# Clustered attention and a maxout network on one core: clusters counted for four heads at once with tokens on partitions, a wide mask, and later gathers

## The chip, the cores and the metric

One core of a Trainium2 chip runs the whole program. The metric is device time in microseconds (us), shown as the median of three runs with the lowest and the highest beside it. The profile is one execution on the same chip, recorded by the hardware profiler; its span runs from the first to the last instruction.

## The reference

```python
# B, H, S, D = 4, 8, 768, 64; C = 16 centroids per head
q_assign = argmax(normalize(q) @ normalize(centroids).T)      # per head, per token
k_assign = argmax(normalize(k) @ normalize(centroids).T)
mask = q_assign[:, :, :, None] == k_assign[:, :, None, :]
scores = where(mask, q @ k.T / sqrt(D), -1e9)
x = softmax(scores) @ v            # 4 x 8 x 768 x 64 -> 3072 x 512 by token
h = maximum(maximum(x @ w1, x @ w2), x @ w3)                  # 512 -> 768
out = h @ w_out                                              # 768 -> 512
```

A query meets only the keys of its own cluster. A head has 16 clusters over 768 tokens.

## The kernel before

**What it computes with.** Each head's tokens are sorted by cluster into eight blocks of 128 places; two clusters share a block, the one of rank r by size and the one of rank 15 - r, one from the block's front and one from its back, so that queries meet keys in eight blocks of 128 x 128 and not in the full 768 x 768. If two clusters that share a block have more than 128 tokens, a flag is set, and a second kernel that does without sorting runs behind it; with the inputs used here it does not. Float32 numbers are carried as pairs of 16-bit ones (a high and a low part).

**Stages of a pair of heads** (`pair_units`). `load_x` (L334 to L339) brings q and k of two heads, transposed, into `stage`. `cluster_scores` (L350) multiplies them by the centroids in a two-bank PSUM tile `big`. `best` (L354 to L370) turns 32 x 32 squares with DVE (L356) and finds each token's cluster as a one-hot row, then counts tokens per cluster. `count` (L373 to L421) is a chain that alternates: TensorE sums counts across partitions (L375, L376, L394, L407, L408, L413 to L415, L419) into one bank of `one`, and DVE makes ranks, mates and the start of each cluster from them in small steps. `places` (L423 to L456) gives each token its place, and copies places between partitions (L450). `fences` (L458 to L468) makes two mask tables. `scales` and `splits` (L472 to L512) scale and split the rows of q, k and v. `scatter` (L515, L518) is twelve indirect DMAs issued by GpSimd (POOL): rows of k and v go to their places in a DRAM buffer, one of a ring of three.

**Stages of a head.** The blocks come back from DRAM as kt (transposed) and vt (L537 to L539). `order_q` (L556, L558, L566) sorts q: DVE makes a one-hot matrix `hot` of 128 x 1024 for each of six tiles, TensorE multiplies, ACT copies to `qt`. `scores` (L580 on) makes, in a `big` tile, for each of eight blocks two matmuls of q by the two parts of k (L587, L588) and one of three rows that adds the mask (L589); DVE takes the row maxima (L591), ACT the exponentials (L596) and a 16-bit copy (L600), DVE the remainder (L601), SP transposes it by DMA into `pt`. `values` multiplies by v (L615 to L617), DVE divides (L620), SP writes `o` to one of three DRAM buffers (L622), and POOL gathers it back into token order with six indirect DMAs (L626), into `xb`.

**The network.** A batch's `xb` is scaled and split (`x_split`, split16 at L237 and L238) and transposed. `ffn_units` makes 18 hidden groups of twelve matmuls (L670), twice a batch, each in a bank of `one`, evicted by ACT (L680) or DVE (L682), and three output groups of 18 matmuls (L702), twice a batch. There are 144 hidden and 24 output groups in the run.

**PSUM** has eight banks: two `big` tiles of two banks each (cluster scores, ordered q, scores), and four of `one` (counts, scales, values, the network).

**What sets the order.** Each unit is put into a plan by head, with a priority, by the numbers in the loop at the end (from L730). The tile scheduler then emits instructions for each engine by these priorities and by its own timeline. A pair's count has a priority of three heads ahead of it, read-back and ordering 1.2 heads ahead. The network of a batch is spread over the eight heads of the next one, and the last batch's runs behind the last head. On each engine instructions run in the emitted order, so that a waiting one holds all behind it; POOL's order of scatters and gathers is fixed this way too.

## Time and profile before

| | |
|---|---|
| median of three runs | 1157.52 us |
| lowest, highest | 1144.28, 1160.65 us |
| the profiled execution's own time | 1155.83 us |
| its span | 1154.0 us |
| mean granted TensorE clock | 0.777 of full speed |
| scatters and gathers on POOL | 192 (L518) and 192 (L626) |

A row of a group reads: line, engine, operation, output<-inputs by the program's names, shapes, count; then busy us in all and mean ns of one; then the idle us of the engine just before these instructions and what ended it. PE is TensorE's matmuls, PEld its weight loads, which overlap them; DVE is VectorE, ACT ScalarE, POOL GpSimd, SP SyncE. "DMA o<-of" names a transfer, "remote" something the profile could not place, "issue" time in which nothing was waited for. The granted clock is a share of full speed. The program has no loops on the chip: every unit is written out, so that a line's count is its number of executions.

### The profile page before, as it was taken

How to read it: one execution, taken by the hardware profiler on the slowest of the kernel's cores; microseconds unless marked ns; L12 is line 12 of the kernel's file. 1: busy time of each engine (PE TensorE's matmuls, PEld its weight loads, DVE VectorE, ACT ScalarE, POOL GpSimd, SP SyncE). 2: the span in 40 equal slices, each digit the busy share in tenths (PEclk: the TensorE clock that was granted, in tenths of full speed). 3: DMA queues.
4: the chain of work that ended last, by engine and by line, in shares of the span. 5: the costliest groups of instructions: out<-in, count | busy, mean ns of one | idle time of the engine just before them, and what ended most of it. 6: DMA issues, size and time to landing. Idle time of an engine off the chain costs nothing.

```text
span 1154.0 us, 13292 instructions
## 1 busy us (share of the span) xinstructions
PE 748.6 (65%) x4409; PEld 388.5 (34%) x4409; DVE 644.4 (56%) x1803; ACT 372.8 (32%) x903; POOL 414.1 (36%) x452
## 2 busy tenths in 40 slices
PE   1426253443475778939577586939687597948996
PEld 1113121221243333515234242615234243524553
DVE  6976878675674645737175564828284553412221
ACT  3243444334242323414160332405160232321111
POOL 4403637273706162352505243251605244250000
PEclk7657575666687777959779597968878697988998
DMA  9564867555753427443484246443483235342000
GB/s 296 185 167 120 210 145 214 129 139 114 172 122 84 109 80 148 100 108 95 128 155 112 58 103 149 100 117 92 125 160 88 57 80 101 82 98 41 1 29 31
DMA packets 273167, 133.93 MB, mean 116 GB/s; under 512 B 234432, under 2 KB 252864, under 8 KB 273088
## 3 DMA queue, kind: packets, MB, share of 16 engines
q1 hardware_dynamic: 257728, 110.95, 41.0%
q0 software_dynamic: 15360, 22.04, 6.5%
q8 instruction: 36, 0.59, 0.2%
q14 instruction: 43, 0.35, 0.1%
HBM read 58.75 MB, written 34.34 MB: 81 GB/s over the span
## 4 chain that ended last, share of the span: by engine, by line
PE 36%; another core or an unknown queue 15%; DVE 11%; issue 5%; DMA 3%; ACT 2%; POOL 1%; SPq 0%; DVEq 0%; ACTq 0%; POOLq 0%
PE one L670 22%; PE one L702 5%; PE big L558 3%; DVE hot L556 2%; PE big L589 1%; DMA x<-xh 1%; PE big L587 1%; PE big L350 1%; DVE nm L591 1%; DMA out_dram<-o 1%; DVE cl_qc L450 1%; ACT e L596 1%; DVE cl_r L370 1%; POOL xb L626 1%
## 5 line engine op out<-in xcount | busy, mean ns | idle before, releaser
L626 POOL DMA_INDIRECT xb<-o,cl_qi x192 | 206.4, 1075 | 501.4 <-DMA o<-of 381.7
L670 PE MATMUL one<-x,w 128*128 128x384 f16 x1728 | 317.5, 340 | 27.1 <-DMA x<-xh 24.8
L558 PE MATMUL big<-hot,q 128*128 128x512 f16 x384 | 135.5, 500 | 175.3 <-DVE hot L556 97.1
L518 POOL DMA_INDIRECT kv<-kv,cl_ki x192 | 194.4, 1013 | 121.9 <-issue 93.1
L670 PEld LDWEIGHTS <-w 128*128 128x128 f16 x1728 | 171.6, 102 | 148.7 <-issue 49.5
L596 ACT ACTIVATE e<-big,nm,sc_al 128x128 f32<-128x128 f32 x256 | 113.0, 461 | 104.6 <-DVE nm L592 76.6
L556 DVE TENSOR_SCALAR hot<-line,cl_qc 128x1024 f16<-128x1024 f16 x192 | 89.9, 494 | 81.8 <-remote 55.2
L558 PEld LDWEIGHTS <-q 128*128 128x128 f16 x384 | 43.8, 117 | 246.8 <-issue 229.0
L587 PE MATMUL big<-kt,qt 128*128 128x128 f16 x256 | 62.3, 243 | 69.4 <-issue 30.7
L566 ACT CAST qt<-big 128x1024 f16<-128x1024 f32 x32 | 32.6, 1019 | 221.0 <-remote 185.8
L591 DVE TENSOR_REDUCE nm<-big 128x8 f32<-128x1024 f32 x32 | 39.0, 1219 | 93.8 <-remote 51.8
L620 DVE TENSOR_TENSOR of<-one,r 128x512 f32<-128x512 f32 x32 | 21.8, 681 | 86.7 <-remote 54.6
L682 DVE SCALAR_TENSOR_TENSOR wf_h<-one,wf_h 128x384 f32<-128x384 f32 x48 | 26.6, 554 | 71.1 <-PE one L670 50.9
L588 PE MATMUL big<-kt,qt 128*128 128x128 f16 x256 | 62.8, 245 | 2.1 <-DMA kt<-kv 2.1
L589 PE MATMUL big<-mask,mask 3*128 3x128 bf16 x256 | 61.8, 242 | 0.0
L350 PE MATMUL big<-stage,cw 128*128 128x512 f32 (+1 forms) x128 | 59.0, 607 | 3.9 <-POOL zero L319 2.7
L702 PE MATMUL one<-wo,vf_h 128*128 128x512 f16 x216 | 56.2, 402 | 6.6 <-issue 6.6
L711 ACT ACTIVATE o<-one,so 128x512 f32<-128x512 f32 x24 | 16.0, 688 | 133.0 <-remote 73.8
L596 ACT ACTIVATION_READ_ACCUMULATOR e<-big,nm,sc_al 128x1 f32 x256 | 53.6, 209 | 0.0
L702 PE MATMUL one<-wo,wf_h 128*128 128x512 f16 x216 | 49.0, 379 | 3.2 <-issue 3.2
L682 DVE SCALAR_TENSOR_TENSOR vf_h<-one,vf_h 128x384 f32<-128x384 f32 x48 | 26.6, 553 | 37.4 <-ACT vf_h L680 20.8
L588 PEld LDWEIGHTS <-qt 128*128 128x128 f16 x256 | 26.2, 102 | 61.3 <-issue 59.7
(205 smaller groups left out, 1120.8 us busy)
## 6 DMA issues: line engine op xcount, KB each, us to landing
stage<-in_qk_dram SPq DMA_DIRECT2D x32, 384.0 KB
wd<-in_moe_w_dram SPq DMA_DIRECT2D x18, 512.0 KB
vt<-kv SPq DMA_DIRECT2D x32, 256.0 KB
o<-of SPq DMA_DIRECT2D x32, 256.0 KB
rows<-in_qr_dram SPq DMA_DIRECT2D x16, 384.0 KB
rows<-in_kr_dram SPq DMA_DIRECT2D x16, 384.0 KB
rows<-in_vr_dram SPq DMA_DIRECT2D x16, 384.0 KB
out_dram<-o SPq DMA_DIRECT2D x24, 256.0 KB
```

What stands on the lines that cost most here:

```text
L350: nc.tensor.matmul(t[:, lo:hi], cw[:, 2 * pr + i, :], d["x"][i][:, lo:hi], start=(i == 0), stop=(i == 1))
L518: i = nc.gpsimd.indirect_dma_start(out=t, out_offset=bass.IndirectOffsetOnAxis(ap=d["ki"][:, n : n + 1], axis=0), in_=d["kv"][:, n].rearra ...
L556: nc.vector.tensor_scalar(a, line, d["qc"][:, h, n : n + 1], None, op0=ALU.is_equal)
L558: nc.tensor.matmul(t[:, lo : lo + 512], d["q16"][:, h * QT + n].rearrange("p a d -> p (a d)"), a[:, lo : lo + 512], start=(n == 0), stop=( ...
L587: nc.tensor.matmul(ts[:, j], q[:, j], k[:, 0, j], start=True, stop=False)
L588: nc.tensor.matmul(ts[:, j], q[:, j], k[:, 1, j], start=False, stop=False)
L589: nc.tensor.matmul(ts[:, j], mq[rows, j], mk[rows, j], start=False, stop=True)
L596: nc.scalar.activation(x[:, j], ts[:, j], AF.Exp, bias=nm[:, j : j + 1], scale=d["al"][:, 0:1], accum_out=sm[:, j : j + 1])
L626: nc.gpsimd.indirect_dma_start(out=xb[b][:, n, h * D : h * D + D], out_offset=None, in_=od, in_offset=bass.IndirectOffsetOnAxis(ap=d["qi"] ...
L670: nc.tensor.matmul(t[:, 0:NB], w16[:, jt, wa, i, ct], x16[b, gi][:, :, xa * CT + ct, :], start=(n == 0), stop=(n == 3 * CT - 1),)
L682: nc.vector.scalar_tensor_tensor(m, t[:, 0:NB], 2.0**-24, ms[jt], op0=ALU.mult, op1=ALU.max)
L702: nc.tensor.matmul(t[:, 0:DM], h16[jt][:, ha, tt * P : (tt + 1) * P], wo16[:, jt, wa, :], start=(n == 0), stop=(n == 3 * JT - 1),)
```

## The change

**Clusters.** `four_units` takes the place of the cluster half of `pair_units`, for four heads at once. The scores of four heads add up in one tile `four`, a two-bank PSUM tile of its own (`one` goes from four banks to two): 128 rows are 4 heads x (q, k) x 16 clusters. ACT copies it out, TensorE transposes six tiles of 128 tokens, so that tokens stand on partitions, and DVE finds the one-hot rows. Counts, ranks and starts then stand one cluster to a partition (L390 to L432 of the new file), with five rounds to TensorE (L392, L397 and L398, L415, L423, and the places). `places` (L439 to L442) adds up the number of earlier tokens of the same cluster by twelve matmuls of up to 512 columns, two DVE steps pick each token's own, and no copy between partitions is needed. The tables and constants for this are made on POOL at the start, and there are more of them.

**Mask.** `fences` makes a table of 32 rows per head; `scores` starts each `big` tile with two matmuls of 512 columns (L631) in place of eight of 128.

**Scatter and gather.** Scatters go out by head, six at a time, into a ring of four buffers of one head. The gather is a unit of its own, put one head later (LATE = 1), with four buffers for `o` instead of three. The network of a batch begins one head later with it. k and v rows are loaded by token, `hot` has two buffers instead of three, `stage` three instead of two, the rows four instead of three; weights are prepared over heads 1 to 12 instead of 0 to 8.

The core of the diff:

```diff
-    ps_one = ctx.enter_context(tc.tile_pool(name="ps_one", bufs=4, space=PSUM))
+    ps_one = ctx.enter_context(tc.tile_pool(name="ps_one", bufs=2, space=PSUM))
+    ps_four = ctx.enter_context(tc.tile_pool(name="ps_four", bufs=1, space=PSUM))
...
-    NRING = 3
+    NRING = 4
...
+    def four_units(b, hf):
+        g = 2 * b + hf
+        d = fours[b, hf] = {}
+        v = nc.vector
+        def small(name, n=1, dt=F32):
+            return sb.tile([P, n], dt, tag=f"s_{name}", name=f"s_{name}", bufs=2)
+        def load_x(i):
+            def f():
+                x = d["x", i] = sb.tile([P, S], F32, tag="stage", name="stage", bufs=NSTAGE)
+                nc.sync.dma_start(out=x, in_=qk[b, 4 * hf + i])
+            return f
+        def cluster_scores(i):
+            def f():
+                if not i:
+                    d["t"] = ps_four.tile([P, 2 * 512], F32, tag="four", name="four")
+                for lo, hi in ((0, 512), (512, S)):
+                    nc.tensor.matmul(
+                        d["t"][:, lo:hi], cw[:, 4 * hf + i, :], d["x", i][:, lo:hi], start=(i == 0), stop=(i == 3)
+                    )
+            return f
+        def best():
+            cs = sb.tile([P, S], F32, tag="stage", name="stage", bufs=NSTAGE)
+            nc.scalar.copy(cs, d["t"][:, 0:S])
+            t = d["t"]
+            for n in range(QT):
+                nc.tensor.transpose(t[:, n * P : (n + 1) * P], cs[:, n * P : (n + 1) * P], ident)
+            s = t[:, 0:S].rearrange("p (x c) -> p x c", c=C)
+            m = sb.tile([P, QT * U], F32, tag="cl_m", name="cl_m", bufs=1)
+            v.tensor_reduce(m, s, axis=AX.X, op=ALU.max)
+            oh = d["oh"] = sb.tile([P, QT, P], F16, tag="cl_oh", name="cl_oh", bufs=2)
+            v.tensor_tensor(
+                oh.rearrange("p n (u c) -> p (n u) c", c=C), s,
+                m.rearrange("p (x o) -> p x o", o=1).broadcast_to([P, QT * U, C]), op=ALU.is_equal,
+            )
+        def ranks():
+            oh = d["oh"]
+            ps = d["ps"] = d["t"][:, S:]
+            own = n_own[:, g : g + 1]
+            for n in range(QT):
+                nc.tensor.matmul(ps[:, 0:1], oh[:, n], ones[:, 0:1], start=(n == 0), stop=(n == QT - 1))
+            nc.scalar.copy(own, ps[:, 0:1])
+            cd = small("cd", C, F16)
+            v.tensor_tensor(cd, delta, ps[:, 0:1].broadcast_to([P, C]), op=ALU.mult)
+            key = ps[:, C : 2 * C]
+            nc.tensor.matmul(key, head16, cd, start=True, stop=False)
+            nc.tensor.matmul(key, ones[0:1], line[0:1, 0:C], start=False, stop=True)
+            tmp = small("tmp", C)
+            mine = n_key[:, g : g + 1]
+            v.tensor_tensor(tmp, key, delta, op=ALU.mult)
+            v.tensor_reduce(mine, tmp, axis=AX.X, op=ALU.add)
+            rk = d["rk"] = small("rk")
+            v.tensor_scalar(tmp, key, mine, None, op0=ALU.is_lt)
+            v.tensor_reduce(rk, tmp, axis=AX.X, op=ALU.add)
+        def blocks():
+            ps, rk, base = d["ps"], d["rk"], n_base[:, g : g + 1]
+            e = small("e", C, F16)
+            v.tensor_scalar(e, order, rk, n_own[:, g : g + 1], op0=ALU.is_equal, op1=ALU.mult)
+            rest = small("rest")
+            v.tensor_scalar(rest, rk, -1.0, C - 1.0, op0=ALU.mult, op1=ALU.add)
+            v.tensor_tensor(rest, rk, rest, op=ALU.min)
+            count = ps[:, 2 * C : 3 * C]
+            nc.tensor.matmul(count, unit, e, start=True, stop=True)
+            tmp = small("tmp8", NJ)
+            v.scalar_tensor_tensor(tmp, order[:, 0:NJ], rk, count[:, NJ : 2 * NJ], op0=ALU.is_equal, op1=ALU.mult)
+            v.tensor_reduce(base, tmp, axis=AX.X, op=ALU.add)
+            full, total = small("full"), small("total", 1, F16)
+            v.scalar_tensor_tensor(full, base, n_own[:, g : g + 1], limit, op0=ALU.add, op1=ALU.is_gt)
+            v.scalar_tensor_tensor(total, full, 1024.0, n_own[:, g : g + 1], op0=ALU.mult, op1=ALU.add)
+            nc.tensor.matmul(ps[:, 4 * C : 4 * C + 1], unit, total, start=True, stop=True)
+            at = small("at")
+            v.scalar_tensor_tensor(at, rest, float(P), base, op0=ALU.mult, op1=ALU.add)
+            off = n_off[:, g : g + 1]
+            v.tensor_scalar(off, ps[:, 4 * C : 4 * C + 1], float(S), None, op0=ALU.not_equal)
+            v.scalar_tensor_tensor(at, off, far, at, op0=ALU.mult, op1=ALU.add)
+            dg = d["dg"] = small("dg", P, F16)
+            v.tensor_scalar(dg, identh, at, None, op0=ALU.mult)
+            d["e"] = e
+        def places():
+            oh, dg, t = d["oh"], d["dg"], d["t"]
+            ts = t[:, 0:S].rearrange("p (n x) -> p n x", n=QT)
+            for lo, hi in ((0, 4), (4, QT)):
+                w = lambda x: x.rearrange("p (o x) -> p o x", o=1).broadcast_to([P, hi - max(m + 1, lo), P])
+                m = -1
+                nc.tensor.matmul(ts[:, lo:hi], ones, w(dg), start=True, stop=False)
+                nc.tensor.matmul(ts[:, lo:hi], before, oh[:, lo:hi], start=False, stop=False)
+                for m in range(hi - 1):
+                    nc.tensor.matmul(
+                        ts[:, max(m + 1, lo) : hi], ones, w(oh[:, m]), start=False, stop=(m == hi - 2)
+                    )
+            x = sb.tile([P, S], F16, tag="cl_x", name="cl_x", bufs=1)
+            v.tensor_tensor(x, t[:, 0:S], oh.rearrange("p n x -> p (n x)"), op=ALU.mult)
+            code = d["code"] = sb.tile([P, QT, U], F32, tag="cl_code", name="cl_code", bufs=3)
+            v.tensor_reduce(
+                code.rearrange("p n u -> p (n u)"), x.rearrange("p (y c) -> p y c", c=C), axis=AX.X, op=ALU.add
+            )
+            idx = d["idx"] = sb.tile([P, QT, U], I32, tag="cl_idx", name="cl_idx", bufs=4)
+            v.tensor_tensor(idx, code, most.rearrange("p n a u -> p n (a u)"), op=ALU.min)
+        def fences():
+            ps, e = d["ps"], d["e"]
+            for i, t in enumerate((first, second)):
+                x = sb.tile([P, 4, NJ, 4], F16, tag=f"rows{i}", name=f"rows{i}", bufs=1)
+                src = e[:, (1 - i) * NJ : (2 - i) * NJ].rearrange("p (a j s) -> p a j s", a=1, s=1)
+                v.tensor_tensor(x, t, src.broadcast_to([P, 4, NJ, 4]), op=ALU.mult)
+                nc.tensor.matmul(
+                    ps[:, 3 * C : 3 * C + 2], x.rearrange("p a j s -> p (a j s)"), (is_qk, is_k)[i], start=(i == 0), stop=(i == 1)
+                )
+            tq, tk = small("tq"), small("tk")
+            v.tensor_scalar(tq, ps[:, 3 * C : 3 * C + 1], q_sign, q_base, op0=ALU.mult, op1=ALU.add)
+            v.tensor_scalar(tk, ps[:, 3 * C + 1 : 3 * C + 2], k_sign, k_base, op0=ALU.mult, op1=ALU.add)
+            mq = d["mq"] = sb.tile([P, P], BF16, tag="mq", name="mq", bufs=2)
+            v.tensor_scalar(mq, q_line, tq, None, op0=ALU.is_ge)
+            mk = d["mk"] = sb.tile([P, NJ, P], BF16, tag="mk", name="mk", bufs=2)
+            v.tensor_scalar(mk.rearrange("p j s -> p (j s)"), k_line, tk, -BIG, op0=ALU.is_ge, op1=ALU.mult)
+        return (
+            [load_x(i) for i in range(4)], [cluster_scores(i) for i in range(4)], [best, ranks, blocks, places, fences]
+        )
...
     def scores(b, h):
         d, i = st[b, h // 2], h & 1
         t = big()
-        k, q, (mq, mk) = d["k", i], d["q", i], d["m"]
+        k, q, four = d["k", i], d["q", i], fours[b, h // 4]
         ts = t.rearrange("p (j s) -> p j s", j=NJ)
-        rows = slice(32 * i, 32 * i + 3)
+        rows = slice(2 * C * (h & 3), 2 * C * (h & 3) + 2 * C)
+        for j in range(0, NJ, 4):
+            mk = four["mk"][rows, j : j + 4]
+            nc.tensor.matmul(ts[:, j : j + 4], four["mq"][rows], mk, start=True, stop=False)
         for j in range(NJ):
-            nc.tensor.matmul(ts[:, j], q[:, j], k[:, 0, j], start=True, stop=False)
-            nc.tensor.matmul(ts[:, j], q[:, j], k[:, 1, j], start=False, stop=False)
-            nc.tensor.matmul(ts[:, j], mq[rows, j], mk[rows, j], start=False, stop=True)
+            nc.tensor.matmul(ts[:, j], q[:, j], k[:, 0, j], start=False, stop=False)
+            nc.tensor.matmul(ts[:, j], q[:, j], k[:, 1, j], start=False, stop=(j % 4 == 3))
...
+    def gather(b, h):
+        d, i = st[b, h // 2], h & 1
+        od = oring[(b * H + h) % NOUT]
         if b not in xb:
-            xb[b] = sb.tile([P, QT, DM], F32, tag="xb", name="xb", bufs=1)
+            xb[b] = sb.tile([P, QT, DM], F32, tag="xb", name="xb", bufs=NXB)
         for n in range(QT):
             nc.gpsimd.indirect_dma_start(
                 out=xb[b][:, n, h * D : h * D + D],
                 out_offset=None,
                 in_=od,
-                in_offset=bass.IndirectOffsetOnAxis(ap=d["qi"][:, i, n : n + 1], axis=0),
+                in_offset=bass.IndirectOffsetOnAxis(ap=d["index"](i, n, 0), axis=0),
             )
...
-    LEAD = 2
     put(0, -3, clear_ring)
     for b in range(B):
+        for hf in range(2):
+            k = b * H + 4 * hf
+            load, mm, rest = four_units(b, hf)
+            at = max(k - 9, 0)
+            for i in range(4):
+                put(at, k - 9 + i, load[i])
+            for i in range(4):
+                put(at, k - 8.5 + i, mm[i])
+            for i, u in enumerate(rest):
+                put(max(k - 5, 0), k - 5 + 0.2 * i, u)
         for pr in range(NPAIR):
             u = pair_units(b, pr)
             k = b * H + 2 * pr
-            at = max(k - 2 * LEAD, 0)
-            put(at, k - 4, u["load_x"])
-            put(at, k - 4, u["load_rows"])
-            at = max(k - LEAD - 1, 0)
-            for i, n in enumerate(("cluster_scores", "best", "count", "places", "scales", "splits", "scatter", "fences")):
-                put(at, k - 3 + 0.05 * i, u[n])
-            put(max(k - 1, 0), k - 1.2, u["q0"])
-            put(max(k - 1, 0), k - 1.2, u["read0"])
-            put(max(k, 0), k - 0.2, u["q1"])
-            put(max(k, 0), k - 0.2, u["read1"])
+            at = max(k - 5, 0)
+            for x in u["load_rows"]:
+                put(at, k - 5, x)
+            at = max(k - 4, 0)
+            for i, n in enumerate(("sums", "scales", "split_kv", "split_q")):
+                put(at, k - 4 + 0.1 * i, u[n])
+            for h in range(2):
+                put(max(k + h - 2, 0), k + h - 2.5, u["scatter"][h])
+                put(max(k + h - 1, 0), k + h - 1.5, u["read"][h])
+                put(max(k + h - 1, 0), k + h - 1.2, u["order"][h])
+    LATE = 1
     for b in range(B):
-        k = b * H + H
+        for h in range(H):
+            k = b * H + h
+            put(min(k + 1 + LATE, B * H), k + LATE - 0.4, gather, b, h)
...
+        k = b * H + H + LATE```

On POOL, before, around the twelfth head; an L626 row is the gather of one head (o_168 serves heads 0, 3, 6 and so on), an L518 row the scatter of a pair, here of heads 16 and 17, then 18 and 19, then 20 and 21:

```order
L626 DMA xb<-o_170,cl_qi 128x64 x6
L626 DMA xb<-o_168,cl_qi 128x64 x6
L518 DMA kv_166<-kv_3722,cl_ki 2048x320 x12
L626 DMA xb<-o_169,cl_qi 128x64 x6
L626 DMA xb<-o_170,cl_qi 128x64 x6
L518 DMA kv_164<-kv_4262,cl_ki 2048x320 x12
```

The scatter of head 16 stands behind the gather of head 12. After the change, with the same heads' scatters; o_227 serves heads 0, 4, 8 and so on, and an L554 row is the scatter of one head:

```order
L675 DMA xb<-o_228,cl_idx 128x64 x6
L675 DMA xb<-o_229,cl_idx 128x64 x6
L554 DMA kv_222<-kv_3161,cl_idx 1024x320 x6
L554 DMA kv_223<-kv_3161,cl_idx 1024x320 x6
L675 DMA xb<-o_230,cl_idx 128x64 x6
L675 DMA xb<-o_227,cl_idx 128x64 x6
L554 DMA kv_224<-kv_3619,cl_idx 1024x320 x6
L554 DMA kv_225<-kv_3619,cl_idx 1024x320 x6
```

The scatter of head 16 (kv_222) now stands behind the gather of head 10, and the gathers of heads 11 and 12 follow the scatter of head 17.

On PE, before, in one of the first heads: the last score matmuls of a head, a count's matmul (L394, with its weights), and the values of the same program step:

```order
L588 LDWEIGHTS qt
L588 MATMUL big<-kt,qt 128x128
L589 LDWEIGHTS mask_582
L589 MATMUL big<-mask_584,mask_582 128x128
L394 LDWEIGHTS unit_108
L394 MATMUL one<-s_dr,unit_108 64x16
L615 LDWEIGHTS pt
L615 MATMUL one<-vt,pt 128x64
```

And after, at the like place, the last score matmul of a head, the count of four heads' matmul (L415), and the ordering of another head's q (L601):

```order
L634 LDWEIGHTS qt
L634 MATMUL big<-kt,qt 128x128
L415 LDWEIGHTS unit
L415 MATMUL four<-s_e,unit 128x16
L601 LDWEIGHTS q_992
L601 MATMUL big<-hot,q_992 128x512
```

The small matmul still stands in PE's queue between a head's scores and the next work, but it does so for four heads at once and writes a bank that nothing else uses; the mask no longer closes the scores.

476 lines of the change are left out of this document (194 added, 282 removed).

## The prediction

> **What bounds the kernel now.** The first view to read is the busy time of each engine, at the head of the page.
>
> ```profile
> PE 748.6 (65%) x4409; PEld 388.5 (34%) x4409; DVE 644.4 (56%) x1803; ACT 372.8 (32%) x903; POOL 414.1 (36%) x452
> ```
>
> No engine is full, so these shares do not name a bound. The stages do. The row maximum of the scores (L591) runs once a head, and its first and last start say when the heads run.
>
> ```profile
> L591 DVE TENSOR_REDUCE nm<-big x32: 1203/1224/1225, 67.2 to 1006.3; 128x8 f32<-128x1024 f32 x32
> ```
>
> Heads run from 67 to 1006 us; what follows is the last batch's feed-forward network alone. The feed-forward work of batch 0 cannot begin before its eighth head is gathered, so I cut at 299 us, where the ninth head is scored, and at 1006 us. The view of busy time by stretch (us busy, instructions in brackets, PE, PEld, DVE, ACT, POOL, then the granted clock):
>
> ```profile
> 67.00:299.00 232.00, 88.88 (x574) 47.09 (x574) 175.08 (x517) 96.42 (x235) 111.12 (x94) 0.63 0.62 157
> 299.00:1006.00 707.00, 523.22 (x3085) 268.73 (x3084) 391.78 (x1087) 226.61 (x576) 259.26 (x261) 0.81 0.47 108
> 1006.00:1154.00 148.00, 114.74 (x670) 62.70 (x668) 30.84 (x53) 26.41 (x57) 17.30 (x18) 0.91 0.17 41
> ```
>
> In the first stage, nine heads in 232 us (25.8 us a head), DVE is busy 75% and PE 38% at a clock of 0.63. In the second, 23 heads in 707 us (30.7 us a head), PE is busy 74% and DVE 55%. So the first stage is DVE's, with PE hanging on it, and the second is nearly PE's. In the second stage I looked for what breaks PE's work, and found that it comes in pieces: while POOL issues the twelve scatters of a pair (L518), nearly every engine stops. Five such windows, then two stretches between them:
>
> ```profile
> 623.00:638.10 15.10, 5.69 (x30) 2.29 (x29) 2.51 (x4) 0.00 (x0) 11.74 (x12) 0.70 0.35 116
> 681.80:697.30 15.50, 9.96 (x57) 3.46 (x55) 0.59 (x1) 0.00 (x0) 12.14 (x12) 0.89 0.17 60
> 749.00:764.10 15.10, 7.03 (x36) 3.25 (x35) 2.19 (x4) 0.00 (x0) 11.69 (x12) 0.71 0.63 171
> 809.90:825.00 15.10, 8.46 (x31) 2.77 (x30) 0.69 (x1) 0.28 (x1) 11.69 (x12) 0.95 0.35 86
> 882.20:897.40 15.20, 3.73 (x13) 1.62 (x12) 3.17 (x6) 0.51 (x1) 11.85 (x12) 0.70 0.33 97
> 655.00:681.80 26.80, 26.80 (x173) 14.95 (x173) 24.47 (x87) 15.20 (x38) 6.02 (x7) 0.91 0.52 111
> 719.00:749.00 30.00, 29.57 (x226) 17.96 (x226) 26.84 (x84) 15.92 (x40) 6.51 (x6) 1.00 0.36 88
> ```
>
> The five windows last 76.0 us, and PE is busy for 34.9 of them (5.69 + 9.96 + 7.03 + 8.46 + 3.73); between the windows PE is full and DVE nearly so. The profile names no cause for this. The waits, over the run (sum, times, longest) and then in the first stage alone:
>
> ```profile
> POOL xb L626 <- DMA o<-of: 381.7, 21, 45.8
> PE big L558 <- DVE hot L556: 97.1, 18, 12.9
> PE one L408 <- DVE s_dv L406: 25.8, 6, 5.3
> PE one L375 <- DVE cl_r L370: 25.3, 12, 6.6
> PE one L394 <- DVE s_r L396: 14.3, 4, 4.4
> PE one L407 <- DVE s_tmp L400: 9.1, 5, 3.1
> ```
>
> ```profile
> PE big L558 <- DVE hot L556: 48.1, 5, 12.9
> PE one L408 <- DVE s_dv L406: 20.5, 5, 5.1
> PE one L394 <- DVE s_r L396: 12.2, 3, 4.4
> PE one L407 <- DVE s_tmp L400: 7.5, 4, 3.1
> ```
>
> PE takes part in each pair's count with small matmuls between chains of small DVE steps, and stands still for 74.5 us at them, 40.2 of these in the first stage. The largest wait, 381.7 us, is POOL's, for an output to land before its gather.
>
> **The change part by part.** DVE first. The costliest and the cheapest of the wide count steps, the copies that turn places round, and the largest and smallest of the small kinds:
>
> ```profile
> L464 DVE TENSOR_TENSOR mask<-side,one 64x1024 bf16<-64x1024 f16 x32 | 37.3, 1203 | 0.0
> L450 DVE COPY cl_qc<-cl_code 32x6 f32<-32x6 f32 x128 | 22.4, 175 | 2.1
> L363 DVE TENSOR_TENSOR cl_e<-cl_e,rank 128x384 f16<-128x384 f16 x16 | 5.6, 353 | 0.1
> L411 DVE TENSOR_SCALAR s_e<-line,s_grp,s_cp 64x8 f16<-64x8 f16 x16 | 4.4, 276 | 0.3
> L420 DVE TENSOR_SCALAR s_kp<-s_kp 64x1 f32<-64x1 f32 x16 | 2.2, 135 | 0.0
> L473 DVE TENSOR_REDUCE sc<-rows 128x1 f32<-128x768 f32 x16 | 15.1, 943 | 4.1 <-DMA rows<-in_vr_dram 4.0
> L556 DVE TENSOR_SCALAR hot<-line,cl_qc 128x1024 f16<-128x1024 f16 x192 | 89.9, 494 | 81.8 <-remote 55.2 <-PE big L558 16.7 <-issue 7.6
> ```
>
> Sixteen wide kinds, from L464 to L363, make 193 us of DVE, and 28 small kinds, from L411 to L420, 76 us: 269 us for 16 pairs, 16.8 us a pair. The new chain has 27 steps for four heads. Its two reductions of 768 elements are costed by L473 (0.94 us each), its two 768-element products at the same, the wide mask step by L556 (0.49) and 22 small ones at about 0.22: 3.8 + 0.5 + 4.9 = 9.2 us, or 73 us in all. DVE loses 196 us.
>
> First stage: five pairs' chains go (84 us) and two and a half new ones come (23), so DVE falls from 175 to 114 us. If all 61 us came off, that is the gain; if DVE stayed at 75% it would be 81 (232 - 114/0.755); if the heads are held by something else, nothing. The 40.2 us of PE's count waits are the part that is visibly on the path. I take **-50**, bounds 0 and -81.
>
> Second stage. Of the count waits, one kind has most of its time there:
>
> ```profile
> PE one L375 <- DVE cl_r L370: 14.7, 9, 3.4
> ```
>
> The other three kinds have 9.0 us outside the first stage together (25.8 + 14.3 + 9.1 - 40.2), some before 67 us. So 14.7 to 23.7 us: **-20** (bounds 0, -24), since a new chain has five hops for four heads instead of four for two, and its PSUM pair delays nobody but itself. The cluster scores no longer take a buffer of `big`, which was waited for:
>
> ```profile
> L587 PE MATMUL big<-kt,qt 128*128 128x128 f16 x256 | 62.3, 243 | 69.4 <-issue 30.7 <-DVE cl_t L356 14.2 <-DMA kt<-kv 13.6
> L589 PE MATMUL big<-mask,mask 3*128 3x128 bf16 x256 | 61.8, 242 | 0.0
> L558 PE MATMUL big<-hot,q 128*128 128x512 f16 x384 | 135.5, 500 | 175.3 <-DVE hot L556 97.1 <-ACT qt L566 44.1 <-issue 33.8
> L670 PE MATMUL one<-x,w 128*128 128x384 f16 x1728 | 317.5, 340 | 27.1 <-DMA x<-xh 24.8 <-DVE wf_h L682 1.2 <-ACT vf_h L680 0.8
> L682 DVE SCALAR_TENSOR_TENSOR wf_h<-one,wf_h 128x384 f32<-128x384 f32 x48 | 26.6, 554 | 71.1 <-PE one L670 50.9 <-PE one L617 15.3 <-PE one L485 2.2
> L601 DVE SCALAR_TENSOR_TENSOR hl<-e,hl 128x1024 f16<-128x1024 f32 x32 | 38.9, 1215 | 4.3 <-ACT hl L600 4.2
>
> ```
>
> That wait, L587 for cl_t, goes: **-14** (0, -14). The mask's 256 matmuls of 61.8 us become 64 of 512 columns, at most 0.5 us each by L558: 32 us. 30 us less, 23/32 of it in this stage, half on the path: **-11** (0, -22). The added place matmuls (3456 columns per four heads at 0.5 us per 512, 27 us), 48 transposes (0.25 each by L587, 12) and some 96 small ones in place of 144 (17 for 26) add 30 us; by the same reckoning **+11** (0, +22). DVE's relief shortens PE's waits for `hot` (97.1 - 48.1 = 49 us outside the first stage), but that tile loses its third buffer: a hot costs DVE 0.49 us and PE two matmuls of 0.35 busy, so two buffers do as long as DVE is not late: **-10** (-49, +20).
>
> `one` keeps two banks of four. A feed-forward group is twelve matmuls, 12 x 317.5/1728 = 2.20 us, and its eviction takes 0.55 us on DVE (L682). With one wide step in front of it (L601, 1.2 us) it comes at 1.75 us and is hidden behind the next group; with two (2.95 us) PE waits 0.75. Three quarters of 144 + 24 groups, 126, run beside heads; with two wide steps in front of every third one, 126 x 0.24 = **+30** (0, +160; the upper end is in the rivals). Fewer short stops should raise the clock a little: 34 us fewer of them, **-12** (0, -99).
>
> The scatters of a head now stand behind the gather of the head six before, instead of four, and the gather itself a head later. What hides this is the scatter's lead: the key and value blocks of a head are still asked for 1.5 heads ahead. If it is used up, the read-back is late, then the scores. The number of scatters and gathers is unchanged, so the windows stay: **0** (-60 if six scatters at a time stop the engines for less, +60 if a read-back is late by 2.5 us a head).
>
> Ends: before the first scatter stand four loads and four heads' count instead of two, and a longer set-up on POOL: **+5** (-10, +20). The gather a head later moves the tail's first x: **+3** (0, +8).
>
> Sum against the profiled execution, 1155.8: 1155.8 - 50 - 20 - 14 - 11 + 11 - 10 + 30 - 12 + 0 + 5 + 3 = 1087.8. The median of the runs, 1157.5, is 1.7 above it: **1089 us**.
>
> **Rivals.** *The clock comes back.* The granted clock is 0.63 where PE waits for counts, 0.81 in the second stage, 1.00 in a stretch without a scatter. If the short waits are what holds it down, PE's 523 us of the second stage shrink to 523 x 0.81 = 424: 99 us instead of the 12 taken, 1089 - 87 = 1002. Against: the scatter windows themselves show 0.70 to 0.95, and they stay. [...]
>
> *Hidden anyway.* The period of a pair in the second stage is 61 us: 15 us of scatter window and 46 us in which PE is full. If the count waits only fill time in which the next scatter is awaited, and the first stage is held by the way scatter, read-back, order, scores, output, gather, then the waits merely change owner. For it: POOL's 381.7 us and the windows. Against: between the windows PE is at 26.80 of 26.80 us, and DVE at 24.5. Gain 20 in the first stage, +8 at the ends: 1146.
>
> *Two banks stall the network* (slower). If each of the 126 groups finds two wide steps (2.43 us), its own eviction (0.55) and ACT's step before that (L680, 0.49) in front, PE waits 3.47 - 2.20 = 1.27 us: 160 us instead of 30, 1089 + 130 = 1219. It decides from the point at which an eviction ends over 2.20 us after its group. For it: DVE is 91% busy between the windows. Against: the change takes just those wide steps (L464 at 1.2 us) off DVE, and its load in the second stage falls by about a third.
>
> **How the numbers follow.** Forecast 0.47, the clock 0.19, hidden 0.17, banks 0.17. The forecast's own spread is 1035 to 1140. A measurement can tell about 2% here, 1134 to 1181. Faster: 0.47 less its top end (0.03) and 0.19, 0.63. Same: 0.17 and 0.03, 0.20. Slower: 0.17. The range reaches past 1002 to 985, where the first stage's low bound also counts in part; upwards past hidden to 1185, half-way into the banks' case.
>
> **What would show it.** DVE busy near 450 us instead of 644, with the first nine heads in about 182 us. PE's waits for counts under 40 us. Scatters of six rows in 7.6 us, with PE less than half busy in them. Waits of L718 (the network's matmul, L670 before) for DVE or ACT tell the banks: under 40 us as forecast, over 120 in the rival. If the second stage keeps 30.7 us a head with those waits low, it is "hidden"; if its clock passes 0.9, the first rival. The prediction is wrong if scores begin to wait for kt (13.6 us before) by more than 60 us.

## The result and the profile after

The kernel before took 1157.52 us (1144.28 to 1160.65), the changed one 961.39 (949.23 to 962.35): a ratio of 0.830, 95% interval 0.819 to 0.841. The forecast was 1089, its range 985 to 1185. The sign was right; the gain was nearly three times what was forecast, and beyond the range. The profiled execution of the changed kernel took 949.23 us.

First the engines, then the first and last row maximum of the heads, then the time by stretch (us busy of PE, PEld, DVE, ACT, POOL, then the granted clock), cut where the first, the ninth and the last head's row maximum starts. All these rows are the changed kernel's:

```profile
PE 706.6 (75%) x4313; PEld 382.8 (40%) x4313; DVE 480.4 (51%) x1185; ACT 378.2 (40%) x921; POOL 428.4 (45%) x476
```

```profile
L636 DVE TENSOR_REDUCE nm<-big x32: 1175/1220/1242, 66.2 to 752.4; 128x8 f32<-128x1024 f32 x32
```

```profile
66.00:220.00 154.00, 87.82 (x527) 44.96 (x525) 104.21 (x270) 85.60 (x208) 89.46 (x82) 0.69 0.84 192
220.00:752.00 532.00, 426.54 (x2673) 230.99 (x2672) 296.16 (x727) 236.24 (x605) 275.59 (x257) 0.86 0.64 145
752.00:947.00 195.00, 160.53 (x997) 89.78 (x995) 43.16 (x77) 35.27 (x72) 31.57 (x33) 0.93 0.23 50
```

The same cut for the kernel before lies at 67, 282 and 1006 us (the prediction cut at 299, 17 us behind the ninth head's row maximum, so that its 232 us held a little under eight and a half heads' steps and not nine):

```profile
67.00:282.00 215.00, 86.71 (x543) 45.20 (x543) 159.66 (x471) 87.09 (x211) 98.88 (x84) 0.64 0.60 153
282.00:1006.00 724.00, 525.39 (x3116) 270.62 (x3115) 407.21 (x1135) 235.93 (x601) 271.50 (x270) 0.80 0.48 110
```

Up to the first head nothing changed (67 and 66 us). Heads 1 to 8 fell from 215 to 154 us, heads 9 to 32 from 724 to 532, and the tail rose from 148 to 195. That is -1, -61, -192 and +47 us, -207 in all between spans of 1154.0 and 947.5. The tail rose because the heads now run faster than the network that is spread beside them: 656 of its 1728 hidden matmuls begin after the last row maximum, where 455 did before. Net of the tail, the late heads gave 145 us.

The waits that answer to those of before:

```profile
POOL xb L675 <- DMA o<-of: 153.9, 16, 17.2
...
PE big L601 <- DVE hot L599: 21.8, 13, 8.6
...
PE four L415 <- DVE s_rest L412: 11.4, 3, 5.7
...
PE one L718 <- ACT wf_h L728: 5.6, 4, 3.2
```

POOL's wait for outputs went from 381.7 to 153.9, PE's for the one-hots from 97.1 to 21.8, those at the count from 74.5 to some 25 (L392, L397, L415 and L423 together; 11.4 of them at L415). The network hardly waits for an eviction (L718 for L728 and L730, 8 us in all, of which the row shows 5.6), so two banks are enough.

### The profile page after: what moved, and what is told of

Read it like the earlier page. It is cut to its first block, busy times and chain, and to the rows that moved or that the text cites. A ratio compares the mean times of both kernels' runs of the same rounds, so it can differ in the third digit from the quotient of the medians.

```text
span 947.5 us, 12743 instructions
## 1 busy us (share of the span) xinstructions
PE 706.6 (75%) x4313; PEld 382.8 (40%) x4313; DVE 480.4 (51%) x1185; ACT 378.2 (40%) x921; POOL 428.4 (45%) x476
## 4 chain that ended last, share of the span: by engine, by line
PE 49%; issue 15%; DVE 14%; another core or an unknown queue 7%; DMA 5%; ACT 4%; POOL 3%; SPq 1%; DVEq 0%; POOLq 0%; ACTq 0%
PE one L718 26%; PE one L750 8%; PE big L601 5%; DVE hot L599 3%; PE four L366 3%; ACT e L641 2%; DVE hl L646 2%; DMA rows<-in_v_dram 1%; DVE nm L636 1%; PE big L633 1%; PE big L631 1%; POOL kv L554 1%; PE big L634 1%; DMA x<-xh 1%
## 5 line engine op out<-in xcount | busy, mean ns | idle before, releaser
L718 PE MATMUL one<-x,w 128*128 128x384 f16 x1728 | 313.4, 339 | 46.0 <-DMA x<-xh 24.2
L675 POOL DMA_INDIRECT xb<-o,cl_idx x192 | 205.7, 1071 | 233.8 <-DMA o<-of 153.9
L554 POOL DMA_INDIRECT kv<-kv,cl_idx x192 | 203.5, 1060 | 170.7 <-issue 112.5
L718 PEld LDWEIGHTS <-w 128*128 128x128 f16 x1728 | 172.9, 101 | 171.7 <-issue 71.8
L601 PE MATMUL big<-hot,q 128*128 128x512 f16 x384 | 126.9, 450 | 37.0 <-DVE hot L599 21.8
L599 DVE TENSOR_SCALAR hot<-line,cl_code 128x1024 f16<-128x1024 f16 x192 | 92.5, 499 | 47.5 <-remote 21.8
L601 PEld LDWEIGHTS <-q 128*128 128x128 f16 x384 | 39.3, 108 | 102.0 <-issue 76.4
L366 PE MATMUL four<-stage,cw 128*128 128x256 f32 (+1 forms) x128 | 57.0, 595 | 16.6 <-DMA stage<-in_qk_dram 11.5
L633 PE MATMUL big<-kt,qt 128*128 128x128 f16 x256 | 44.2, 249 | 15.6 <-issue 8.7
L634 PE MATMUL big<-kt,qt 128*128 128x128 f16 x256 | 44.3, 249 | 11.2 <-issue 10.2
L646 DVE SCALAR_TENSOR_TENSOR hl<-e,hl 128x1024 f16<-128x1024 f32 x32 | 39.1, 1223 | 16.2 <-ACT hl L645 11.6
L660 PE MATMUL one<-vt,pt 128*128 128x64 f16 x256 | 31.7, 203 | 20.5 <-issue 15.3
L636 DVE TENSOR_REDUCE nm<-big 128x8 f32<-128x1024 f32 x32 | 39.0, 1218 | 14.7 <-remote 11.6
L366 PEld LDWEIGHTS four<-stage,cw 128*128 128x128 f32 x128 | 28.9, 234 | 42.8 <-issue 24.1
```

The costliest lines, as they stand in the source:

```text
L366: nc.tensor.matmul(d["t"][:, lo:hi], cw[:, 4 * hf + i, :], d["x", i][:, lo:hi], start=(i == 0), stop=(i == 3))
L554: i = nc.gpsimd.indirect_dma_start(out=ring[at], out_offset=bass.IndirectOffsetOnAxis(ap=index(h, n, 1), axis=0), in_=d["kv"][:, h * QT + ...
L599: nc.vector.tensor_scalar(a, line, code, None, op0=ALU.is_equal)
L601: nc.tensor.matmul(t[:, lo : lo + 512], d["q16"][:, h * QT + n].rearrange("p a d -> p (a d)"), a[:, lo : lo + 512], start=(n == 0), stop=( ...
L633: nc.tensor.matmul(ts[:, j], q[:, j], k[:, 0, j], start=False, stop=False)
L634: nc.tensor.matmul(ts[:, j], q[:, j], k[:, 1, j], start=False, stop=(j % 4 == 3))
```

## The experiments

Comparisons are made with the kernel before on the same chip. This matters here, because the kernel before itself took 1143 to 1157 us on four occasions, on different chips, and 995 and 990 us on two others. The changed kernel itself was not run on the chip of experiments 1 to 4; by its ratio elsewhere, 0.830 and 0.835, it would take 949 to 955 us there. Times below are medians; "heads 1 to 8" and so on are read from the starts of the row maxima.

**1. DVE's time given back** (changed kernel, `a_dve`).

```diff
+    def dve_load():
+        x = sb.tile([P, NJ], F32, tag="dummy", name="dummy", bufs=2)
+        for n in range(6):
+            nc.vector.tensor_reduce(x, k_line.rearrange("p (j s) -> p j s", j=NJ)[:, :, 0:96], axis=AX.X, op=ALU.max)
+    for k in range(B * H):
+        put(k, k - 2.2, dve_load)
```

> The changed kernel with six row maxima over 768 elements added to DVE for each head, 192 in all, whose results nobody reads: at 0.75 to 0.94 us each they put 145 to 180 us back on DVE, about what the new cluster count took off (644 to 480 us). Nothing waits for them but what stands behind them on DVE. If DVE's work is what the gain comes from, in the second stage too, the time rises by 100 us or more, to 1060 or above. If the gain comes from the scatters, the gathers or the PSUM pair, it rises by less than 40 us.

1040.86 beside 1143.66 us for the kernel before, some 90 us over the changed kernel's 949 to 955, between the two marks. The added steps, the heads' row maxima, and the added steps between the ninth head's row maximum and the last (us, steps, then the granted clock):

```profile
L806 DVE TENSOR_REDUCE dummy<-k_line 128x8 f32<-128x768 f16 x192 | 177.0, 939 | 0.6 <-POOL k_line L170 0.6
```

```profile
L636 DVE TENSOR_REDUCE nm<-big x32: 1205/1214/1225, 97.2 to 840.8; 128x8 f32<-128x1024 f32 x32
```

```profile
309.00:841.00 532.00, 43.64 (x47) 0.87 0.59 134
```

177 us of DVE cost some 90. All of it lies early: the first row maximum comes at 97 us instead of 66, heads 1 to 8 take 212 us, as long as before the change (215), and heads 9 to 32 take 532, as without the steps. But the added steps lie early too, since they wait for nothing: 54 of the 192 stand before the first row maximum, 91 in heads 1 to 8 (84 us) and only 47 (43.6 us) in heads 9 to 32. So in the first heads DVE's time counts, as forecast: 84 us more of it cost 58. In the late heads of the changed kernel DVE has room for 44 us more. That is a fifth of what the old cluster work of twelve pairs took (12 x 16.8 = 202 us), and more was not tried there.

**2. Twelve scatters in a row again** (changed kernel, `a_ring6`).

```diff
-    NRING = 4
+    NRING = 6
-                put(max(k + h - 2, 0), k + h - 2.5, u["scatter"][h])
+                put(max(k - 2, 0), k - 2.5 + 0.01 * h, u["scatter"][h])
```

> The changed kernel with a ring of six one-head buffers instead of four, and both scatters of a pair at one priority, so that twelve scatters again go out in a row. If the twelve in a row are what stops the engines (PE 46% busy in windows of 15 us before, about 80% in windows of 7.6 us after), the time rises by about 60 us, to 1020, and the windows are again 15 us with PE half idle. If the windows stood still only because DVE or PE waited for something else, the time stays within 15 us of 961.

957.98 us, ratio 0.833 (0.826 to 0.839): no loss. The windows are of 15 us again. Three of the worse ones, and then three windows of six scatters in the changed kernel:

```profile
555.10:570.20 15.10, 4.63 (x38) 2.36 (x37) 1.52 (x4) 5.87 (x19) 11.71 (x12) 0.75 0.19 62
608.70:623.80 15.10, 5.62 (x49) 3.34 (x47) 6.15 (x17) 4.18 (x14) 11.75 (x12) 0.79 0.28 94
660.60:675.70 15.10, 3.74 (x40) 2.05 (x39) 1.05 (x3) 4.63 (x17) 11.74 (x12) 0.76 0.19 62
```

```profile
522.80:530.50 7.70, 7.70 (x38) 4.37 (x37) 2.80 (x7) 5.06 (x18) 6.18 (x6) 0.95 0.91 196
556.80:564.30 7.50, 4.51 (x44) 2.21 (x41) 1.01 (x4) 2.42 (x5) 5.91 (x6) 0.79 0.18 59
570.30:577.80 7.50, 7.50 (x38) 3.45 (x36) 4.42 (x22) 5.89 (x19) 5.94 (x6) 1.00 1.09 175
```

PE stands still for two thirds of such a window again, and the whole is as fast as before the edit: what is lost in the windows is made up between them. Twelve scatters in a row, with a ring of six, cost nothing here, though the windows look worst in the profile. What six buffers are worth by themselves was not tried, and they may hide a cost.

**3. The gather soon again** (changed kernel, `a_soon`).

```diff
         nc.sync.dma_start(out=od.rearrange("(j p) d -> p j d", p=P), in_=x)
+        gather(b, h)
...
-    LATE = 1
+    LATE = 0
...
-            put(min(k + 1 + LATE, B * H), k + LATE - 0.4, gather, b, h)
+            pass
```

> The changed kernel with the gather put back at the values of its own head, and the network one head earlier. If the later gather made the gain (POOL's wait for outputs fell from 381.7 to 153.9 us), that wait rises to 300 us or more and the time by 40 us or more. If POOL's wait was off the path, the time stays within 15 us; a network that starts earlier could even take some us off the tail.

997.12 us, ratio 0.875 (0.870 to 0.879): 42 to 48 us slower. POOL's wait for outputs stayed at 146.6 us, so the later gather is not what shortened that wait. What it costs stands at a change of batch; POOL's instructions there:

```profile
507.75 1.45 POOL L676 DMA_INDIRECT xb<-o,cl_idx  x1 [0.30 <-issue]
540.32 1.13 POOL L676 DMA_INDIRECT xb<-o,cl_idx  x1 [31.12 <-DVE vf_h L731]
```

The second row is the first gather of the third batch. It waits 31 us, the scatters behind it wait too, and the row maxima of two heads stand 74 us apart (502 and 576). The profile puts the wait down to a step of the network (L731). By the trace, the output that it gathers landed at 539.45 us, 0.9 us before it starts, as with the 21 gathers of the kernel before that waited over 2 us for theirs (0.85 to 0.92 us); the `xb` that it writes had its last reader, the split of the batch before, at 520.2. So it waits for its own output. That comes late because on PE the first 68 matmuls of the network of the batch before (L719) stand in front of the values that make it (L660 to L662):

```profile
517.40 5.56 PE L719 MATMUL one<-x,w 128*128 128x384 f16 x24 [1.24 <-DMA x<-xh]
532.10 0.19 PE L660 MATMUL one<-vt,pt 128*128 128x64 f16 x1
```

At the change of batch before it, the first gather waits 32 us, and its output too landed 0.9 us ahead. The edit moves the network one head forward together with the gather, so the loss belongs to both.

**4. The mask in eight narrow steps** (changed kernel, `a_narrow`).

```diff
-        for j in range(0, NJ, 4):
-            mk = four["mk"][rows, j : j + 4]
-            nc.tensor.matmul(ts[:, j : j + 4], four["mq"][rows], mk, start=True, stop=False)
         for j in range(NJ):
-            nc.tensor.matmul(ts[:, j], q[:, j], k[:, 0, j], start=False, stop=False)
-            nc.tensor.matmul(ts[:, j], q[:, j], k[:, 1, j], start=False, stop=(j % 4 == 3))
+            nc.tensor.matmul(ts[:, j], q[:, j], k[:, 0, j], start=True, stop=False)
+            nc.tensor.matmul(ts[:, j], q[:, j], k[:, 1, j], start=False, stop=False)
+            nc.tensor.matmul(ts[:, j], four["mq"][rows], four["mk"][rows, j], start=False, stop=True)
```

> The changed kernel with the mask added by eight matmuls of 128 columns a head, last in each block, as before, with the 32-row tables. My sum gave the wide mask 11 us in the second stage and something like 4 in the first: 960 to 980. A rival, that the mask can be done ahead of kt and so shortens the way from kt to the maximum, gives 30 us or more.

987.36 us, ratio 0.861 (0.856 to 0.865): 32 to 38 us slower. The profiled execution is 40 us longer, with 27 of them in heads 1 to 8 (181 us instead of 154) and 10 in heads 9 to 32 (542 instead of 532). That is twice what I gave it. That it is the mask's place ahead of kt that counts, as the rival has it, fits but was not tried apart.

**5. The changed kernel again** (`after2`, no edit).

> The changed kernel once more, so that the runs of this chip have it beside them: 0.83 of the kernel before, within 0.82 to 0.84.

966.35 us, ratio 0.835 (0.828 to 0.843).

**6. No cluster work from the fifth pair on** (kernel before, `b_nocount`, and again as `b_nocount2`).

```diff
         def count():
+            if g >= 4:
+                nc.gpsimd.memset(flags[:, g], 0.0)
+                return
...
         def places():
+            if g >= 4:
+                for n in ("qc", "qi", "ki"):
+                    d[n] = st[0, 3][n]
+                return
```

and the like in `load_x`, `cluster_scores`, `best` and `fences`.

> The kernel before, but from the fifth pair on (heads 8 to 31) without loads for clusters, cluster scores, best, count, places and fences; these heads use the places and masks of the fourth pair. If the old cluster work, by its waits on PE and its turn in the two big tiles, is what made the heads from 8 on slow, they fall from 725 us to 600 or less, and the whole to 1030 or less. If the plan, the scatters and the early gathers made them slow, they stay above 680.

> The kernel before without cluster work from the fifth pair on, again. Where the kernel before takes about 1150 us, 0.88 of it as before. Where it takes about 995: if the work itself costs, it falls by 60 us or more there too; if only the standstill made it dear, by less than 30.

1018.45 beside 1156.97 us, its four runs between 994 and 1024, so 0.86 to 0.88; and 875.56 beside 990.36, ratio 0.882 (0.879 to 0.886). The share is about the same on both kinds of chip. The old cluster work of twelve pairs costs some 12% of the kernel, 115 to 139 us by the medians; my sum had 34 for its waits in the late heads. The profiled execution on the first chip takes 616 us for heads 9 to 32, where 600 or less was expected. These edits take out the work on DVE, PE and the queues all at once, and the indices are there from the start, so they do not tell which of these costs how much.

**7. The cluster scores in a PSUM pair of their own** (kernel before, `b_own`).

```diff
-    ps_one = ctx.enter_context(tc.tile_pool(name="ps_one", bufs=4, space=PSUM))
+    ps_one = ctx.enter_context(tc.tile_pool(name="ps_one", bufs=2, space=PSUM))
+    ps_four = ctx.enter_context(tc.tile_pool(name="ps_four", bufs=1, space=PSUM))
...
-            t = d["t"] = big()
+            t = d["t"] = ps_four.tile([P, 2 * 512], F32, tag="four", name="four")
```

> The kernel before with two banks of one instead of four, and the cluster scores of a pair in a two-bank tile of their own instead of a big one. My sum has +30 for the banks and -14 for the shared tile: 1150 to 1180. If the cluster scores' turn in the two big tiles is what holds scores and ordered queries apart (an odd head's query was ready some 50 us before its scores), it falls by 60 us or more, to 1090 or less.

1132.37 us, ratio 0.982 (0.975 to 0.989): 21 us faster by the ratio, where +16 was in the sum.

**8. The later gather alone** (kernel before, `b_late`): the gather as a unit of its own one head later, NOUT = 4, values after scores.

> The kernel before with the gather one head later as a unit of its own, four output buffers, values after scores, and the network one head later, all else as it was. Putting the gather back in the changed kernel cost some 45 us, nearly all about the changes of batch. If that is a gain by itself, this kernel is faster by 30 to 50 us; if it only counts once the heads run closer, or the tail gives it back, it stays within 15 us.

1131.03 us, ratio 0.978 (0.969 to 0.986): 26 us faster, a little under what was expected. By the profiled executions 8 us of it lie in heads 9 to 16 and 15 in heads 17 to 32, and the first gathers of the third and fourth batch still wait 30 and 36 us. The differences of experiments 7 and 8, 2%, are no larger than what a changed order of instructions alone can do (28 us in experiment 9).

**9. The waits cut, the work kept** (kernel before, `b_dvefree`, `b_pefree`, `b_bothfree`, and the last again as `b_bothfree2`). For pairs from the fifth on, `rd` and `rr` are kept copies of the fourth pair's results:

```diff
+            use = lambda n, x: keep[n] if g >= 4 and PEFREE else x
+            rd = keep["ps"] if g >= 4 and DVEFREE else ps
+            rr = use("r", d["r"])
...
-            own, tot = ps[0:M, 0:C], ps[0:M, C : 2 * C]
+            own, tot = rd[0:M, 0:C], rd[0:M, C : 2 * C]
```

> The kernel before with all its cluster work on every engine, but from the fifth pair on DVE's cluster steps no longer read what PE has just made: they read a kept copy of the fourth pair's results (and its transpose is a pass over the kept one in place), so these heads use the fourth pair's counts. PE still waits for DVE. Leaving the old cluster work out of heads 8 to 31 took about 130 us off the whole. If that is DVE standing in line behind PE, with the one-hots and maxima of other heads behind it, this kernel takes most of it back, 60 us or more. If it is work or PE's own waits, less than 25 us.

> The kernel before with all its cluster work, but from the fifth pair on PE's small matmuls of the count take kept copies of the fourth pair's operands (and the fourth pair's q, k and centroids are loaded again), so that PE never waits for DVE in a count; DVE still waits for PE. The waits named for these matmuls from head 8 on add to some 24 us: by my sum 20 to 30 us faster. If PE standing in line is the larger part of the cost, with the rest of the heads' work behind it, 60 us or more.

> Both of these edits together: the same instructions, with no wait between PE and DVE in a count from the fifth pair on. If the waits in both directions are the cost of the old cluster work, this kernel is as fast as the one without that work, some 130 us under the kernel before; if DVE's and PE's time for the work matters, it stays 50 us or more above that.

> The kernel before with no wait between PE and DVE in the counts from the fifth pair on, again. Where the kernel before takes about 995 us, it was 0.997 of it and should be so again. Where it takes about 1150: if the old counts' waits are what the standstill makes long, 60 us or more faster; if the standstill costs what it costs whatever waits, within 25 us.

These fell on chips where the kernel before takes 995 and 990 us. Ratios 1.001 (0.998 to 1.004), 0.968 (0.960 to 0.975), 0.997 (0.994 to 1.000) and 0.998 (0.995 to 1.000). PE's waits alone gave 34 us, somewhat over its named 24, but not when DVE's were cut as well. The traces show why this is no clean price: each edit also changes the order that the scheduler emits. The first scatter of the fourth pair, in `b_pefree` and then in `b_bothfree`:

```profile
195.68 1.00 POOL L544 DMA_INDIRECT kv<-kv,cl_ki  x1 [9.09 <-issue]
```

```profile
224.23 1.01 POOL L544 DMA_INDIRECT kv<-kv,cl_ki  x1 [0.30 <-issue]
```

In the kernels whose DVE steps do not wait, the last index of the fourth pair comes at 216 us instead of 194, with the fifth pair's at 226 close behind it, and the ninth head's row maximum comes at 296 instead of 268. The edit loses these 28 us before the heads that it is meant for. From there to the last row maximum `b_bothfree` takes 544 us and `b_pefree` 539, against 477 in `b_nocount2`. What the kernel before takes there on such a chip isn't known, for none was profiled. So my estimate is that cutting the waits of the count is worth some 3% at most (34 us in `b_pefree`, or the 28 lost in `b_bothfree`); leaving the work out gave 12%. It was not tried on the other kind of chip.

**10. One engine's cluster work left out** (from `b_bothfree`; `b_nodve` skips DVE's steps, those of the places too, so that its indices are there from the start; `b_nope` skips PE's matmuls and their loads).

```diff
+            if g >= 4:
+                from types import SimpleNamespace
+                nc.gpsimd.memset(flags[:, g], 0.0)
+                no = lambda *a, **k: None
+                v = SimpleNamespace(scalar_tensor_tensor=no, tensor_tensor=no, tensor_reduce=no, tensor_scalar=no, tensor_copy=no)
```

> The kernel with no waits in the count, and from the fifth pair on DVE's cluster steps left out; PE still makes the cluster scores in a big tile and the count's small matmuls, on kept operands. If DVE's time is the cost, about 0.89 to 0.91 of the kernel before; if PE's time and its turn in the big tiles is, 0.96 or more.

> The same, but with PE's cluster scores and small matmuls (and the loads for them) left out from the fifth pair on, and all of DVE's cluster steps kept, on kept results. If DVE's time is the cost, 0.97 or more of the kernel before; if PE's time and its turn in the big tiles is, 0.92 or less. If both are about 0.94, each has half.

993.15 us, ratio 0.868 (0.863 to 0.873), and 1072.54, ratio 0.940 (0.932 to 0.947), beside 1143.27. DVE's steps are the larger share: heads 1 to 16 take 391 us without them, 468 without PE's work, 468 in the kernel before (profiled on another chip of that kind). From head 17 to the last row maximum both take 382 to 389 us, against 471 before: there the two kernels gain alike, though `b_nope` keeps all of DVE's steps. What they have in common is that no count links PE and DVE. Whether cutting the links alone would do so on such a chip stays open.

**11. The network earlier** (changed kernel, `a_early`, and `a_early2` beside `after3`, the changed kernel itself).

```diff
-            spread(units, k + 1, min(k + H + 1, B * H), 0)
+            spread(units, k + 1, min(k + H, B * H - 2), 0)
```

> The changed kernel with the network of a batch spread over one head less, and over three less for the third batch. The changed kernel leaves 656 of 1728 hidden matmuls for after the last head, where the kernel before left 455, and its tail is 195 us instead of 148. If PE has room beside the heads (some 105 us idle from the ninth head on), more of them go there and the time falls by 15 to 30 us; if the heads then only run later, it stays within 10 us.

> The changed kernel once more beside the kernel before. Where the kernel before takes about 995 us: if the gain comes from the standstill during scatters, it is 0.93 to 0.98 of that; if it comes from the cluster work itself, 0.83 to 0.88. Where the kernel before takes about 1150: 0.83 again.

> The changed kernel with the network spread over fewer heads, now beside the changed kernel itself on one chip: 10 us or more below it if PE has room beside the heads, within 10 us if not.

`a_early` 902.48 us beside 994.88 (0.906, 0.899 to 0.914); on another chip 897.67, and the changed kernel 853.36, beside 990.36: 0.908 (0.904 to 0.913) and 0.862 (0.859 to 0.864). The earlier network is 44 us slower than the change as it is, and its tail is no shorter (202 us and 193). No version tried beats the changed kernel. `after3` also answers the question of the chips: where the kernel before takes 990 us, the change is worth 0.862, where it takes 1150, 0.83. So most of the gain is there on both kinds.

## Why the prediction was wrong, point by point

**DVE's work: right.** The new chain has 27 steps and 71.4 us in all, 8.9 a group of four (9.2 forecast). DVE fell to 480 us, where about 450 was named as the sign; the other 30 I have not traced.

**Heads 1 to 8: right.** -61 us for -50. In experiment 1, 84 us of DVE steps put into these heads, where the change had taken 55 off (160 to 104), return 58 of them. The bound of 61 for "all of it" was the better value, and the mask has a share in it that I had not seen (27 in experiment 4); the two overlap.

**"The count waits left: -20 (bounds 0, -24)" was the step that failed.** It priced the old cluster work in the late heads by the time that PE was seen waiting for it, and put the rest of what that work takes, on DVE above all, at next to nothing. The waits themselves were not far off: cutting PE's gave 34 us (`b_pefree`, on a chip where the kernel before takes 995). But the work left out gives some 12%, 115 to 139 us (experiment 6). A wait list charges a stretch to whoever comes last, and here that was mostly someone else (`hot`, the outputs, "issue"). The change puts a new count in the place of the old, so 115 to 139 is more than its own part can be known to be. How the work may reach the heads shows on POOL. Scatters of the kernel before, with DVE's last index step, L456, ahead of one (the third pair, in the first heads):

```profile
136.90 0.68 DVE L450 COPY cl_qc<-cl_code 32x6 f32<-32x6 f32 x4
137.62 0.48 DVE L456 TENSOR_SCALAR cl_ki<-cl_code,kbase 64x12 int32<-64x12 f32 x2
```

```profile
139.01 1.00 POOL L518 DMA_INDIRECT kv<-kv,cl_ki  x1 [4.06 <-issue]
```

For each of the 16 pairs the first scatter starts 1 to 8 us after L456 has made the last index, and the chain from L356 to there takes 35 to 50 us for 16.8 us of work (the first pair's, 25), since other heads' steps stand between. From the seventh pair on, the scatter starts 0.3 us behind the gather before it, and that gather, or one just ahead of it, had waited 26 to 46 us for an output, which is also DVE's (L620). So in the late heads the output comes last and the index last but one. In the changed kernel, an index step for heads 17 to 20 and the first of their scatters:

```profile
336.33 0.19 DVE L452 TENSOR_TENSOR cl_idx<-cl_code,most 128x48 int32<-128x48 f32 x1
```

```profile
358.37 1.01 POOL L554 DMA_INDIRECT kv<-kv,cl_idx  x1 [0.31 <-issue]
```

Their other scatters start at 374, 407 and 423 us. From the ninth head on, the indices of four heads are there 12 to 55 us before the first of their scatters, so DVE's counting is no longer the last to arrive, or the last but one. Without DVE's cluster steps (`b_nodve`) POOL waits for the split of k and v instead, again on DVE, but a pair is done in 54 us from the tenth on, where the kernel before takes 66:

```profile
509.69 1.03 POOL L558 DMA_INDIRECT kv<-kv,cl_ki  x1 [14.03 <-DVE kv L552]
```

That what stands ahead on DVE is the mechanism is one reading, and it is not shown for the late heads. Experiment 6, heads 1 to 16 of experiment 10 and the first heads of experiment 1 fit it. Against it, `b_nope` keeps DVE's steps and does a pair in 52 us from the tenth on; in its counts DVE no longer waits for PE, nor PE for DVE. Early indices alone do not start a scatter: in `b_bothfree` the last pair's are there at 653 us and its scatter starts at 778. How the 12% divide between DVE's time, PE's time and the links between them stays open.

**The shared tile and the banks: -14 + 30.** Wrong in sign taken together, and small: -21 (`b_own`). The rival in which two banks stall the network fell, with 8 us of PE's waiting for evictions in L718.

**The gather: 0.** Wrong: 26 us done alone, 42 to 48 undone, with the network moved along in both. Undone, the loss lies about the changes of batch; at the one looked at, PE works on the network before the values whose output the gather needs. The sum looked at the scatter's place behind the gather, and not at the order on PE. POOL's single wait of 37.5 us for L682 in the kernel before was a hint: that gather starts 0.9 us after its own output has landed, so it belongs to the waits for outputs, whatever the row names.

**The mask: -11.** It gives 32 to 38, most of it in the first heads (27) and 10 in the late ones.

**The scatter windows: 0.** Not refuted by experiment 2, though not for a reason I had. The sign named for it, PE less than half busy in windows of six scatters, did not come: in the three shown PE is busy for 7.70 of 7.70, 4.51 of 7.50 and 7.50 of 7.50 us.

**The clock: -12.** The late heads' clock went from 0.80 to 0.86. Their PE work, 525 us, would be 488 at the new clock, so 37 rather than 12 if it all lay on the path. That fewer short stops raise the clock was an estimate; no run shows it apart. The rival had 0.9 as its mark; the clock stopped short of it.

**The ends: +5 and +3.** -1 and +47. The tail was the one large error against the change: faster heads leave more of the network behind, which a sum over the head stage must take back.

So of the 145 us net in the late heads, to which the sum gave 26 (-20 - 14 - 11 + 11 - 10 + 30 - 12), the cluster work is the largest candidate (the 115 to 139 of experiment 6, less what the new count costs), and the gather has 26 to 48. The parts overlap and do not add up exactly.

## What to carry to other kernels

A list of waits names who came last; it does not price the one who was nearly last each time. Where an engine that is busy half the time (DVE here: 56% of the span, 51% after the change) delivers the indices, the operands and the outputs of a pipeline, leave its work out in an experiment before pricing it by waits. Price a faster stage together with what was spread beside it, for that work comes back in the tail. And before moving a gather on a queue, ask what stands in front of the work that makes its source, on the engine that makes it; when a row names a step with no tie to the waiting instruction, look up when the operand itself landed.

## What the hardware showed

The kernel before took 1157.5, 1143.7, 1157.0 and 1143.3 us on some chips and 994.9 and 990.4 on two others, the changed kernel 961 and 966, and 853. One difference can be seen in the scatter windows. In two windows of `b_bothfree2`, on a chip of 990 us, PE is never idle:

```profile
594.00:610.00 16.00, 16.00 (x104) 8.26 (x104) 10.10 (x22) 7.61 (x23) 12.65 (x12) 1.00 0.78 165
635.00:651.00 16.00, 16.00 (x121) 9.21 (x120) 12.56 (x31) 9.13 (x26) 12.65 (x12) 1.00 0.68 157
```

On the others the engines can stop. In the kernel before, on a chip of 1157 us, POOL issued twelve scatters from 681.8 to 697.3 us. The last matmul of a head's values, then the DVE steps that follow, with the division that reads those values:

```profile
684.11 0.19 PE L617 MATMUL one<-vt,pt 128*128 128x64 f16 x1
```

```profile
681.17 1.22 DVE L601 SCALAR_TENSOR_TENSOR hl<-e,hl 128x1024 f16<-128x1024 f32 x1
699.75 0.69 DVE L620 TENSOR_TENSOR of<-one,r 128x512 f32<-128x512 f32 x1 [17.36 <-remote]
```

L620 waits for PE's semaphore alone, and L617 is recorded as done at 684.30 us. In this trace that semaphore moved at 675.82 and next at 699.73, 699.78, 699.83, 699.87, 699.91 and 699.96, the first of these 2.4 us behind POOL's last scatter: six steps in 0.23 us, though the three matmuls of L558 among those that raise it take 0.38 us each and are recorded from 686.94 to 688.18. L620 starts 15.4 us after the end recorded for L617: what was late is the word of PE's being done, not its work, as far as this trace can tell; the wait is named "remote". In the kernel before, the semaphore stands still for over 8 us, while two or more matmuls that raise it are recorded, 11 times, 166 us in all, some 150 of them while POOL issues scatters or gathers; in the changed kernel, run beside it, 11 times, 116 us in all, 107 of them so. The same kernels on the two kinds of chip: DVE's row maximum waits for "remote" 11.6 us (4 times) in the changed kernel and not at all in `after3`, 68.0 us (5 times) in `b_nocount` and not at all in `b_nocount2`. A caution: 38 of 513 raises in the kernel before and 63 of 534 in the changed one are not in the trace, so some of these stops may be of the record alone. And the kind of chip is not all: PE is busy for 79% of the scatter windows from 220 us on in the changed kernel, in the kernel before for 49%. Why some chips show it and others not, no run here tells.
